# Gated linear attention and a low-rank mixer on one core: the second batch in whole chunks, the first batch's u transposed in PSUM, and a new order

## The chip, the cores and the metric

The kernel runs on one core of one Trainium2 chip. The time is device microseconds of one execution, and the number compared is the median of several. The engines are named as the profile names them: PE is TensorE, DVE is VectorE, ACT is ScalarE, POOL is GpSimd, SP is SyncE, which here only issues DMAs.

## The reference

For four batches, eight heads, 768 steps and head size 48, a recurrent state is decayed and updated at each step and read by the query. The result, laid out as (batch, step, 384), goes through a low-rank mixing over the steps (rank 32) and then a two-layer MLP with a residual:

```
state = alpha[:, :, t, :, None] * state + k_t v_t^T
y[:, :, t] = q_t state
h = (x^T U V)^T                       # x = y as (4, 768, 384)
u = x + h
out = u + max(u @ w_ch1, 0) @ w_ch2   # 384 -> 1536 -> 384
```

## The kernel before

**The recurrence.** The steps of a batch are cut into six chunks of 128. In a chunk, ACT takes Ln of alpha (`ln`), PE sums it over the steps (`cum`, or `pcum`), ACT takes Exp of the sum and of its negative (`exp`, twice) and of the total (`tot`, `ptot`). POOL or DVE scale k and q with these (`rk`, `rq`), PE transposes them (`tr`) or a DMA does (`tkq`, batch 3), PE forms the scores (`sc`, `psc`), DVE masks them, and PE multiplies them with v and adds the part from the state (`y`, or `pyi` and `py`). The state goes on through `d`, `add` and `st`. A *paired* chunk works on half of the heads for 256 steps, two steps to a partition, so that its loads read runs of 384 bytes where a whole chunk's read 192. `PAIRS` says how many blocks of 256 steps of each batch are paired: before, three in batch 0 and two in batch 1. Paired chunks have their own forms of the steps (`stage_pair`), whole chunks theirs (`stage_gla`).

**The mixer.** `stage_mix` forms x^T U (`xu`, copied out as `utx`), multiplies it with V for each chunk (`hb`), adds x on DVE (`u`), and transposes u into `uT`, by PE and a copy (`utr`, `uev`) in batches 0 and 1, by DMA (`tu`) in batches 2 and 3. `mlp1` multiplies w_ch1 with `uT` in 24 groups of three matmuls of 384 columns (two halves of the steps, twelve groups of outputs); each group fills a PSUM bank, which a `relu` on ACT or DVE empties. `mlp2` takes twelve matmuls per chunk; DVE adds u (`out`), and a DMA stores.

**The order.** PSUM has eight banks, and each step that makes PE results takes one. All steps of all batches are listed first (`Plan.add`), each with its number; then `Plan.run` issues them in the order of `TABLE`, three characters for each entry: two for the number of the step, one for its engine (P, A, D, G, S); `++` puts filler matmuls on PE. `SLOTS` gives the buffers. The framework's own scheduling is off, so each engine works in the order of `TABLE`, and the batches run into each other: the recurrence of the next batch lies between the MLP matmuls of the present one. One of the steps, listed last, is

```
P.add("table", lambda e: nc.scalar.preload_act_table_set("natural_log_exp_and_others"))
```

It names the set of ACT's function tables that has both Ln and Exp. In the `TABLE` of before it is ACT's third entry, behind two DMA issues.

Of the kernel before, what the change touches and what calls it, by code (L numbers as in the profile page):

```python
# [15 lines left out]
TABLE = """  # L16
ArA++BAASAvSA-AA3SQPAAySAsSCLA++BCNPAtSAzA++BA5ACOACPAAwS++BCiADSAECAAxSBAACRGAuS++BCSGCjACQACkPA4SClA++BCmAA7ADUPDVADWA
A0SC5ACTPCoGCUPCWABDSDXAEEPEGAA6SCpDA9ACVDCxPC7P++BCnACMAC9AAFGC+ABBSDrAA2SCyDCqPCsDCaPBHSCbDCXPCzPEFAA8SCrPCYDDtPCtAA1S
CcPCZDCeP++BCdDC8ADYGDaPCuPDZDCfPEIGDcAC-GDTGCwDEKPEHAAJPDbPC0DBCABFSABSDhPGCAAKADwA++BChACvDDiPDdDDjDEJGDvADuAA+SDePDgD
AGPELPAHADkPEMDC1PDfDBEAENABGSC2PBLSC3DDyGD0PD2ABISCgDBJSBKSBPSGEPDlDC6GGGADIPDJPDKDEOPDxGDLPDAGGHAEDGDBPC4DDzPDnPERPEPD  # L20
GFAAMSDMDALGDCPDDADmPDoPEQDESPD1AAQSDEABMSGJGDpAD3PGZAETDD5DDFPEUPDGDGIGDqAGbPDNPEVPGDGDOPD6P++BDsAGcADHDEWPEXAD4DD7PD8D
DPPDRAEYDGKPGMAD9PAYSGLPGNDACGADPD+PD-PEADGRPGSDDQAAEAEBAGOPGPDEZPEaPBTSGfGGwAGeAGdAEbAGyPG1ABNSGTD++BG0AEqPGQDBRSEoPGhP
GVPErDEkPGgGGWPGzABQAEcPEiPGjAEpDElDGiPGaGEsPHJAAUSAOGGXAEePEjDEtAAPGGkDGYAEdDHLPBOSHMAHNAEfDEmPGlPEnDANGGoPEgPGpDFGPGmD
GqDFHDFIPATABVSGnDFKPARGEhAFLAEwPExAASGFMPFNAE4PE2PAaGFQPE5DEyPBXSG2GBUSAZAFRDAbAFAPFJAE0PAcSE3ABSABZSFEPFFAGrDHOAG4PG6A
G3DHPDE1DFBAEuPHRPHTDFOPHQGEzDFPDG5PHiAFcPAXAFaPEvDG7AFdAAVAHSPHUDGsPGtPGuDBYSGvAG8PG+DAWGAhSBWSGxGGUGBaSAmSHVPBfSBrSG-P
FbAHkPHmAHoAFWPHADHBGE6PHXDH4AHnAFSPHlAG9DHqGFYPFTDH6PE7DH7AH8AHWDE+PHsPHuDHCDHpGE8PHKAFXAFZAHrPHtDFUPFVABbSE-AE9DHEPAgA
HFPHGPHYPHZDAfGBtSBjSHHDHvPHdPHIDHwDH+GIAPFCPAeGHaGAdAH9GHePFePHbDAiABcSHcDHxDICDFDAFkPF2PH-PIBDF8PIDPAlAHfPAjGAkGF9PBeS
HgAFwPBhSIFDHDGIEDHjABnSHyPH2PH3AH5AHzDH0DF3PFlPH1DIGPHhAApAFfPIHAIIPFxPIJAIQPISPAoGIKPAnGIRDITDAqGF+PFyPILDIMPINDFgPIYP
IZDF-DFzDF4PKCAKEPLBABkSIWPKFABzSJuAIXDIUPIOPIVAIPDKXAFmPFnDIaPBqSIbDJwPJxAF5DJ1DIiPKZPJvAIjAKdAI0PBlSFhDKGABdSAIGJyAJEP
JFABvSB1SIgPKKGJ2GI1AI+PI-AKIAIyPI4PKsAI5AIzAJGPIhDBiSI6PI7AJ0AJzAImPIqPKHAIrAInAKaAJKPIwPKDGJ+PJHAIkPKbAKuPKwAJIPLDPJLD  # L30
KcAKMPJ-DLWABwSJAPJJAIuPKyAJBAKfGIlDKeDKvAIxDBgSKJGLGAI2PI3DLHAIvAIcPLEABsSLIGIdAIePIfAKgPKiDJ3PBpSB0SIoPBmSJ5DLFAIpANFA
KxAIsPKhPItAJ4PKODKjAKSPKTDKLPJSPJTPJ6DBoSK0GJ7PLJGKNAB6SBySKUGKtGJ9DKkPKlDKPPKRDJUPLYPLZANHPKmDNJANKAKYGFqPFrPNNGKzGLKP
I8PNLAJ8DNIAKQDKnPBxSLaALcGKqPLMALLPLbDKoDKpGLNAB-SFsPK2PLdPK4DI9AKVPFtDK8PLfABuSK9DKrAJCPJDAK1PK3DLePNMGLgACDSK+GKAPKWA
JkPB3SB2SKBDB7SJVDB5SNWALOPNOSLPDK5PK6DLhPOMAJlPLQDK7DLCGLRPLSDLTGJmPNYPOOPCISORALXAN6ACESNbANoANcAJePLjDLUPLiDNaAK-PLAD
LVDJpPLkPJfPLlANZANPPNeGLmPLnAN8PN9ANGGN-ANQDJqPB4SLvPLtPN+ANRDOAANdGJrPCHSLwDOQALqPCCSLuDCASLxSLrDNXAOeALoPJYPLpDJMPNSP
NTDLsSJgPB8SJZPCFSL0PL1DJhDJsDJaPNqPNtALyPLzDCBSL2SJbDJNPJOPB9SB+SNsAJnDJPDOUGNjPNkDN7AL5PMNPNUPL6ANVDL3PNrAMDPMEANvDMOA
L4ANlGMFPOBDL9PMHPMIAOPAL-PMAAOCDODSNuAMGAOgPOhAL+AMLPMJPMKDMBPOTGOVSOiANwDMbPMTPCJSNfSMUAL7PMcDMfPMPPMCAMgDNpAMMAMVPMWD
MXPMYDOHPOSAOEPMhPOFDOjGL8DMjPMkAN1PN2DOGDOkGMdPMRPMSDNxSMZPCGSMQDMeDMnPN3GOIDOKPOJGOlSMoPMiAGBSOWPOLACKSNyPMaAOXDNgPFjS
NzDNhDNAPNBPMpPONAN0DOZPOmPNiDFpSN4PM2POaDM3POYDN5AOcPOdANmPMlPFvSObGOnDOfGOoDNnDOpPOqAMxPOrPOsAMyPGASMqDMrSMmDM4PO3PO4D
OyPO5PJWSFuSO0PO1DM7POtPNCPOzDO2SM8PM9PM5DO6DO7SOuDMzPM+DJdSOvPOwDOxSMsPMtPMuPPiPNDDPkPPoPPpAPaPPbAPcPPWPPXDPdDF0SM0DFiS  # L40
PMPPNAPCPPDDM1SPlANESPgPPjAPePPAPPGPPhDPOPPYPPBAPKPPLDPSPJoSPTAPUPPVDJjSMvDO8PJiSO9APEPPPDPHAPqPPrDPIPO+PPZAQFPJQSPfDQGP
QKPPmPMwSP7PP8PPnDQLPF7SJRSPFAM-SF1SO-DPxPQHPPJDPQPPRDM6SP2PP3PF6SP4PJcSP5DJtSFoSQMPQNDPsPPyPPzPJXSQIDQJSP0DP6SP1SQOSPtP
P9PP+DP-SPuPQAPQBPPvDPwSQCPQDDQES
"""
SLOTS = """
ABCDEFAAGHIAAJBCAKLAMAABNBBOCCCPBDBEAQBFARSGHACBBDTCUAEBDCVBBGAWEADXBBCEGACDCACBEAFAYZHACAFCCCaGBCAHDDbcBdBAAefghEDAGHDB
CBEAFGDAAEBBiCHABABFCDCEBABGFABCCCDHGFACBHBAGjACDCADAkABFlAEHACGCmBDDFCAABEACnAADGFBAHAECBADABGHAEFBBDDGHCFACDBBFEAHABCD
EGBEHABGEJFCHKEBGCDDBDAACEBCCHCAGECAADHFMEBDHBNOCAFCAGDCEBBLDCHDAGDIFPBAQDGBBBDGBEDGBEDRTAGBSEAUCDABAWFXEBYDADCABCZbBVCF
caHBACBFCCeHAAFCBHEEGAFBACBAAdEDDABfAGACgCEHBGhiDlACCAHECGACBkDDFmnDDAAGCHEBCAFACAABEGCFjBADDCBCBHEBCAGCDACFHACBEDFEGJHB
GFACHABECABBBDGHKBACMDBFAACBCEBBADEAGAEACOBEAICBALPCCAGBEAAVQGecACGZSfgCUhAFABCGBAADCECBCBFBBEDGCDBEBBACNCBFGDACEFDHBBAC  # L50
BFBAAXCCADDDHBlGFADECBAAHGDFEBHFBCCEGDHBaFACGBHFAkjBCEdGFAHBAiFHAFBGDEHABFHABHCGDEBAFEDCCnBGHH
"""
# [99 lines left out]
def kernel(  # L152
# [215 lines left out]
    def stage_pair(b, u, sprev, xb):  # L368
# [160 lines left out]

        def f_y(e):  # L530
            for h in range(HP):
                for j in range(2):
                    for c in range(2):
                        r = slice(64 * c, 64 * c + 64)
                        nc.tensor.matmul(  # L535
                            yb[c]()[:, h * D : (h + 1) * D], lhsT=pm()[r, (h // 2) * 2 + j, h % 2, :], rhs=rv()[r, HP * j + h, :],
                            start=(h == 0 and j == 0 and before[c] is None), stop=(h == HP - 1 and j == 1), skip_group_check=True,
                        )
# [286 lines left out]
    P.add("table", lambda e: nc.scalar.preload_act_table_set("natural_log_exp_and_others"))
# [31 lines left out]
```

## Time and profile before

| | |
|---|---|
| median of 3 runs | 158.62 us (157.86 to 159.13) |
| profiled execution, first to last instruction | 156.8 us |
| PE busy | 148.8 us, 1715 matmuls |
| DVE busy | 107.6 us, 236 instructions |
| ACT busy | 90.0 us, 234 instructions |
| POOL busy | 61.4 us, 95 instructions |
| DMA packets | 98291, of these 91968 under 512 B |

The profile's page gives only the span of the profiled execution; the median of the runs is 1.8 us longer than it. In the rows below, a group is a line of the kernel, an engine and an operation, the tile written and the tiles read, a count, then the busy time and the mean of one in ns, then the idle time of the engine ahead of them and what ended it. The chain is the work that ended last, followed back from the end; its pieces have a start, a length and a name. Rows of stretches give the length, and for each engine the busy time and the number of instructions, then the granted clock of PE, the DMA share and GB/s.

### The profile page before, as it was taken

To read this page: it belongs to the slowest core of one execution; us is meant where nothing else is said; L and a number is where in the kernel's file an instruction comes from. 1 tells how busy PE (TensorE), PEld (TensorE's weight loads), DVE (VectorE), ACT (ScalarE), POOL (GpSimd) and SP (SyncE) were. 2 spreads that over 40 slices of the span, in tenths; PEclk is the share of its full clock that TensorE was granted. 3 is DMA by queue.
4 is the path that set the end of the run, shared out by engine and by line. 5 is a ranking of instruction groups with operands and counts; after the bars stand their busy time and mean duration, and the time that the engine had idled before them with its cause. 6 is when DMAs were issued, how large, how long until landed. Compare 5 with 4: busy or idle time off the path is not lost.

```text
span 156.8 us, 4413 instructions
## 1 busy us (share of the span) xinstructions
PE 148.8 (95%) x1715; PEld 97.7 (62%) x1715; DVE 107.6 (69%) x236; ACT 90.0 (57%) x234; POOL 61.4 (39%) x95
## 2 busy tenths in 40 slices
PE   2878999999999999999999999999999999999992
PEld 0456678666767656666668666665667555556662
DVE  6038899987899628816588976885989580673162
ACT  3678889986978272999958585379232202450000
POOL 8285995756088600136679261052623000000000
PEclk9999999999999999999999999999999999999999
DMA  5999999999988989989989996897976346345625
GB/s 145 319 323 326 268 301 313 344 265 268 280 239 193 270 161 191 189 169 211 208 169 214 134 222 119 169 181 145 176 144 151 105 87 139 127 129 151 199 100 201
DMA packets 98291, 31.53 MB, mean 201 GB/s; under 512 B 91968, under 2 KB 98240, under 8 KB 98272
## 3 DMA queue, kind: packets, MB, share of 16 engines
q1 hardware_dynamic: 92464, 29.11, 80.6%
...
q14 instruction: 6, 0.05, 0.1%
...
## 4 chain that ended last, share of the span: by engine, by line
PE 84%; DMA 8%; DVE 4%; ACT 1%; issue 1%; ACTq 0%; DVEq 0%
PE ps L791 30%; PE ps L765 29%; DMA io<-in_alpha_dram 8%; PE ps L716 3%; PE ps L620 3%; PE ps L592 2%; PE ps L687 2%; PE ps L428 2%; PE ps L535 2%; PE ps L558 2%; PE ps L682 1%; PE ps L736 1%; PE ps L452 1%; PE ps L643 1%; PE ps L702 1%; DVE rkq L411 1%
## 5 line engine op out<-in xcount | busy, mean ns | idle before, releaser
L791 PE MATMUL ps<-w_sb,h1t 128*128 128x384 bf16 (+2 forms) x300 | 53.1, 319 | 0.0
L765 PE MATMUL ps<-uT,w_sb 128*128 128x384 bf16 x288 | 51.0, 326 | 0.1
L775 ACT ACTIVATE h1t<-ps 128x384 bf16<-128x384 f32 x58 | 27.2, 509 | 19.1 <-PE ps L765 19.0
L791 PEld LDWEIGHTS <-h1t 128*128 128x128 bf16 x300 | 27.3, 97 | 15.9 <-issue 0.6
L765 PEld LDWEIGHTS <-w_sb 128*128 128x128 bf16 x288 | 27.0, 98 | 16.3 <-issue 0.4
L777 DVE TENSOR_SCALAR h1t<-ps 128x384 bf16<-128x384 f32 x38 | 20.1, 552 | 19.4 <-PE ps L765 15.9
L579 POOL TENSOR_TENSOR rkq<-io,aa 128x384 bf16<-128x384 f32 x12 | 11.7, 975 | 23.0 <-ACT aa L569 13.2
L630 DVE TENSOR_TENSOR pm<-ps,maskc 128x512 bf16<-128x512 f32 x28 | 17.7, 681 | 2.8 <-PE ps L620 2.8
L717 DVE TENSOR_TENSOR ub<-xb,ps 128x384 bf16<-128x384 bf16 x24 | 12.2, 549 | 6.9 <-PE ps L716 6.9
L797 DVE TENSOR_TENSOR io<-ub,ps 128x384 f32<-128x384 bf16 (+2 forms) x25 | 12.9, 531 | 3.7 <-PE ps L791 3.6
L277 ACT CAST xb<-ps 128x192 bf16<-128x192 f32 (+1 forms) x21 | 8.2, 393 | 10.6 <-PE ps L687 7.9
L463 DVE TENSOR_TENSOR pm<-ps,maskp 128x512 bf16<-128x512 f32 x20 | 13.2, 682 | 0.5 <-PE ps L452 0.2
L277 ACT COPY kqt<-ps 128x512 bf16<-128x512 bf16 x18 | 10.5, 608 | 1.6 <-PE ps L428 0.8
L579 POOL TENSOR_TENSOR rkq<-io,ai 128x384 bf16<-128x384 f32 x9 | 8.2, 914 | 6.9 <-PE ps L643 3.9
L411 POOL TENSOR_TENSOR rkq<-io,ai 128x384 bf16<-128x384 f32 x9 | 8.5, 945 | 6.1 <-ACT lt L380 3.1
L568 ACT ACTIVATE ai<-ps 128x384 bf16<-128x384 f32 x14 | 7.0, 502 | 5.6 <-PE ps L560 3.1
L654 POOL TENSOR_TENSOR st<-sm,tot 128x384 bf16<-128x384 f32 x8 | 6.9, 868 | 8.2 <-DVE sm L670 8.0
L571 ACT ACTIVATE tot<-ps,off 128x4 f32<-128x4 f32 x22 | 5.6, 279 | 5.3 <-PE ps L560 3.4
L279 DVE COPY kqt<-ps 128x512 bf16<-128x512 bf16 x18 | 7.3, 417 | 1.4 <-PE ps L592 0.9
L428 PE MATMUL ps<-ident,rkq 128*128 128x128 bf16 x80 | 8.0, 228 | 0.1
L281 POOL CAST w_sb<-h1t 128x384 bf16<-128x384 f32 x14 | 6.8, 516 | 2.9 <-DMA h1t<-in_moe_w_ch_dram 2.9
L411 POOL TENSOR_TENSOR rkq<-io,aa 128x384 bf16<-128x384 f32 x7 | 6.4, 910 | 3.4 <-ACT aa L404 2.3
...
## 6 DMA issues: line engine op xcount, KB each, us to landing
...
```

The source lines that it names most:

```text
L277: nc.scalar.copy(dst, src)
L411: eng.tensor_tensor(jh(dst()[:, :, 0:D]), raw(a), jh(x()), op=ALU.mult)
L428: nc.tensor.matmul(dst, lhsT=ring()[:, HP * j + 2 * a : HP * j + 2 * a + 2, :].rearrange("t h w -> t (h w)"), rhs=ident, start=True, stop= ...
L463: nc.vector.tensor_tensor(dst, s2, maskp.to_broadcast([C, 2, 2, C]), op=ALU.mult)
L579: eng.tensor_tensor(dst()[:, :, 0:D], a(), x(), op=ALU.mult)
L630: nc.vector.tensor_tensor(pm()[:, :, par, :], s2, maskc.to_broadcast([C, HP, C]), op=ALU.mult)
L717: P.add(f"u {b}.{c}", lambda e, c=c, hb=hb: nc.vector.tensor_tensor(ub()[:, c, :], xb()[:, c, :], hb()[:, 0:DM], op=ALU.add), r=[hb] + xk( ...
L765: nc.tensor.matmul(hb()[:, 0:TW], lhsT=w1_sb[:, ct, jt * 128 : (jt + 1) * 128], rhs=u_half(uT, ct, tt, b in QUEUE_U), start=(ct == 0), sto ...
L775: nc.scalar.activation(dst, hb()[:, 0:TW], AF.Relu)
L777: nc.vector.tensor_scalar_max(dst, hb()[:, 0:TW], 0.0)
L791: nc.tensor.matmul(hb()[:, 0 : hi - lo], lhsT=h1()[:, jt, c * C : (c + 1) * C], rhs=w2_sb[:, jt, lo:hi], start=(jt == 0), stop=(jt == NJ - 1),
L797: P.add(f"out_{hi - lo} {b}.{c}", lambda e, hb=hb, lo=lo, hi=hi: nc.vector.tensor_tensor(flat(ou)[:, lo:hi], ub()[:, c, lo:hi], hb()[:, 0 ...
```

## The change

- `PAIRS` of batch 1 goes from 2 to 0: all its chunks are whole.
- Batch 0 (`INPLACE`) no longer forms u. x is transposed by matmuls with the identity into PSUM (`xt`), the low-rank part is added to the same bank by one more matmul (`ht`), and a copy makes `uT` of it (`xtev`). In the second MLP, a matmul of V and `utx` opens each bank (`hbo`), and `out` adds x where it added u.
- In paired chunks, `py` is two steps, one for each parity of the heads.
- `utx` has three buffers where it had two.
- `TABLE` and `SLOTS` are new.

```diff
-    PAIRS = {0: 3, 1: 2, 2: 0, 3: 0}
+    PAIRS = {0: 3, 1: 0, 2: 0, 3: 0}
+    INPLACE = (0,)
...
-    utxs = Pool(slots("utx", 2, [128, DM], BF16))
+    utxs = Pool(slots("utx", 3, [128, DM], BF16))
...
-        def f_y(e):
-            for h in range(HP):
+        def f_y(e, par):
+            for h in range(par, HP, 2):
...
-        P.add(f"py {b}.{u}", f_y, r=[rv, (pm, 0), (pm, 1)], w=[yb[0], yb[1]])
+        for par in range(2):
+            P.add(f"py {b}.{u}", lambda e, par=par: f_y(e, par), r=[rv, (pm, par)], w=[yb[0], yb[1]])
...
+        if b in INPLACE:
+            for tt in range(2):
+                for j in range(NCT):
+                    tb = Buf(bank)
+
+                    def f_xt(e, tt=tt, j=j, tb=tb):
+                        for n in range(NT):
+                            nc.tensor.matmul(tb()[:, n * C : (n + 1) * C], lhsT=xb()[:, tt * NT + n, j * C : (j + 1) * C], rhs=ident, start=(n == 0), stop=False, skip_group_check=True)
+
+                    P.add(f"xt {b}.{tt}.{j}", f_xt, r=[x for n in range(NT) for x in xk(b, xb, tt * NT + n)], w=[tb])
+                    P.add(
+                        f"ht {b}.{tt}.{j}",
+                        lambda e, tt=tt, j=j, tb=tb: nc.tensor.matmul(tb()[:, 0:TW], lhsT=utx()[:, j * C : (j + 1) * C], rhs=ve_sb[:, tt * TW : (tt + 1) * TW], start=False, stop=True, skip_group_check=True),
+                        r=[utx, ("ve", tt)], w=[tb],
+                    )
+                    P.add(f"xtev {b}.{tt}.{j}", lambda e, tt=tt, j=j, tb=tb: copy(e, uT()[:, j, tt * TW : (tt + 1) * TW], tb()[:, 0:TW]), r=[tb], w=[(uT, "t", tt, j)])
+            return utx
...
+            if b in INPLACE:
+                P.add(f"hbo {b}.{c}", lambda e, hb=hb, lo=lo, hi=hi: nc.tensor.matmul(hb()[:, 0 : hi - lo], lhsT=(ve_sb if paired(b, c) else vm_sb)[:, c * C : (c + 1) * C], rhs=utx()[:, lo:hi], start=True, stop=False), r=[utx, ("ve" if paired(b, c) else "vm", c // NT)], w=[hb])
...
-                            start=(jt == 0), stop=(jt == NJ - 1),
+                            start=(jt == 0 and b not in INPLACE), stop=(jt == NJ - 1),
```

What the new `TABLE` says can be read by counting the steps in the order in which `Plan.add` lists them. Fillers go from 11 to 5. DMA issues on ACT go from 11 to 16. ACT's Ln (L) and Exp (E) entries stand in these runs, with a bar where PE gets the first `mlp1` entry of batch 0, 1, 2 and 3:

```
before  TABLE L1 E2 L3 E5 L1 E5 L1 E3 L1 E6 L1 E1 L1 E5 L1 E2 | E1 L1 E2 L1 E4 L2 E1 L2 E1 |
        E4 L1 E7 L1 E6 L1 E7 L2 E1 L1 E1 L1 E8 L1 E2 | E6 |
after   L2 E1 L1 E2 L1 E9 L1 E2 L1 E4 L2 E6 L1 E2 | E3 L1 E3 L1 E5 L1 E3 L2 E7 L2 E3 L2 |
        E8 L1 E4 L1 E4 L1 E1 L1 E1 L1 E8 L1 E4 | E4 TABLE |
```

TABLE marks the `table` entry, 220th of ACT's 232 entries in the new order.

More of the change, by code (lines that the diff above doesn't have):

```diff
@@ L16 @@
 TABLE = """
[L17 to L40, printed above, removed]
@@ L41 @@
-PMPPNAPCPPDDM1SPlANESPgPPjAPePPAPPGPPhDPOPPYPPBAPKPPLDPSPJoSPTAPUPPVDJjSMvDO8PJiSO9APEPPPDPHAPqPPrDPIPO+PPZAQFPJQSPfDQGP
-QKPPmPMwSP7PP8PPnDQLPF7SJRSPFAM-SF1SO-DPxPQHPPJDPQPPRDM6SP2PP3PF6SP4PJcSP5DJtSFoSQMPQNDPsPPyPPzPJXSQIDQJSP0DP6SP1SQOSPtP
-P9PP+DP-SPuPQAPQBPPvDPwSQCPQDDQES
+AASA3ADVA++CDXPAvSCjAClPAFGAJPDYAArSA4SAGPA5SCLACNPDZADbDCmADdPDcGDePAzSC7AC9PDaACPAAKDCOACQACoAAwSCpGAHDAtSCSGC-AAuSCMG
+DgDAySCkGCnADfDDAADhPDiDDjD++CCyPCrPA-SC+AEHAEJPCUPCWAAsSEKACRGCzDA6SA0SDBGDWGELACtDA1SDCGC0PC1DA7SDvACaPCbDCTPCVD++BDDP
@@ new lines @@
+DFDDkPDlPDmDCcPCXPCZDDEPCdDCYDCePAxSA2SDnPC8ADGAEMADxPBBSCqGCsPDoDDHPDIDBASD0ADKPEOGDLPDMDENGCfPCgPA9SDyACuAA8SD1GDzAD2G
+ChAEQPEPPDQPDNPERACiADPPDJDA+SCvPBCSESDDRPDSPDUADTAEZPDODETPDpPBDSEIGD3PCxDCwDD4PGOAEVDEUDBHSD5ADqPEWPEXPEYDDrPDsPGQPD+P
+DtDAIGD6AGiADuAD7PD8DEaPBFSABSEbPDwGD-PEADC2PC3PC4PGSAGUAGTAGRAC6AC5AEcPEBPGkPACGADPECPAEAD9DEDPEEPGnAEGAEFAGlAElPBESGVG
+EdDEfPGXPEeDEgPEhAGWDAYSAaAGZDEuPGYPAMSAPGErPEoPGaDEsPEvPEtAEmPBLSG3AEpPEqAAZGEwDEiPGmAExPEyPEzDAOGEjPEkDGbPG5PG6AANAAbG
+FgPFhABGSG8AG9AAUSAWGFePGcDFiPFOPEnDFGPBJSAVGBPSFHDBMSAXGGoAFIPE0PE4PGqGFfAFPDFjAHMAFKPE1DG7AE5DGdDFAPHOPGPAGePFBDFLAGfD
@@ new lines @@
+BISBKSFYPFJAFMPHPAGgPHSAG+GGpDBTSHhAE2PFZDHAPFNAHRAE3AHQAGrPFcPFdDGtDGjAGsPGuDBNSG-GHCAAQSATGHjPHnAFaPFbAARGHBPHDDASGBQS
+GyPHmAFEPFFABOSHlAGhABXSBRSH2AGzDHkAGvPGwDHEPHGDFQPE6PFUPFRDE7AHTGHVPE8PG4AFVAFSPFTAE+PH4PH5AALGHUGHFDFCPHWPE9DG0GHXDHKP
+BUSHoGH6AFDAAcSAfAE-AAgGFWPGxDAeGBZSF5PBVSAdAFXAHLDH8GFrPHYDHqPHHPBYSHZPHbDHaDAhSG1PBWSBSAFsPGHPGIPAmAH+PHpDG2AHIDHrPHtD
+IAAAiAAjAF6PH7GHsDH9PH-DFkPFlPIBPICDBaSHuPHvDHwDAkGAlGFmPF7PGJPHJDHNAHcPHdDHeDHiGHxPHyDHzDIDDBbSBfABhAFtPHfPBjSBcSApAFyP
+FzPF0PAnABrAAoGBnSAqGFnPH0PHgDH3GIEPJ8AB3SFoDBgSFuPGAPBdABuSBvSH1DIFAIGPIHDFvDF8PF9DJoAJqPJuAJrAIUPIVDGKPIWPIXDGLDIQPJ+P
@@ new lines @@
+BpSIOPIPDF1PBiAJ-AKAAKBAIYPIIPIRDGBPJtAKCABoAKmAF2DIJDIZAK7AIKPILDGCPISPGDPKoPBkSBeAB5SKEGJsAKpAKDGITDIMPINDKsAKGPKIDKFP
+KHDLQAKRAIyPIzAImPGEDIiPInDIcPB-SBsSKrAJwGK9PK-AJ9GKtGJpGJvDIjDKqAKuGJyPIdALSPI+PI6PI2PI3DIoPBwSIaPLAAI-DJ0DJCPJ4PK+ALBA
+J5DIwPBlSI7AIpALTALUAIxDJDDNQAIkPB6SBtSBxSKMPKwPKvPKxDKNDIlAKTPJxPJzDIbAI0PI8PKVAKZGIsPKUACHAKYGI1AKWAKXAKyDKOGI9DLWGItA
+KJPBqSKKDJ1PJ2DKLDKzPBmSN0AJ3DBySIgPIhAIuPIvACCSJGPB2SIePNSPNUALCGNVAK0DIfDLYPIqPIrAI4PK1DI5ACASGMSBzSKbPKPPKaPKdDCFSKcD
+JPPLaDLDGKSGLVGJHAJ6PJ7DKQDFxSB0SB7SJEPB4SKhPKiDNAANWANTAB+SB1AJQPLXPLZDKjDJAPLFPLHAJBAKnGK2PNRGK3DK4GLEPLGDJFAJRPJSDK5P
@@ new lines @@
+LbPLIPM-ACBALdDKePGNSCGSK6AJKPJLPJMPNBPKfDB9ANEAKgDKkPLcDLJDLRGOYANCANiANFAN2PN5ANDAKlANYGK8GLLPNXGNZSJUPLKDLOPJVPN4ANGG
+LMDLNDLePLPDJIPJJANMPOaPOcACDSLfDJNDNdPLgPLhAObANNDNeDNfDJZPNHGJaPN3ALuPN6ALvDLnPLoDLiPN8GJWPNjGOGALjDLsPLtDJXDJjPLpPNkP
+NISNmANlANnANoALqDLkPJbPLlDJcDJkPJlPNaPNJPN7GN9SN+PJePNcDOADJmDOIPJfPNbDJgPLrSLwSMbPNKDNLDLmSB8AOKANgPMJPOJAN-DNqGMKDL1P
+MZPL5PL2DMcDMXPMYDL6DCJSCESNhAMaANOPNPDOLACIANpGNvPJhDJTSNrSMFPOOGMHPMDPMEAONDLxPOHGLyAMGAOdGOeGLzPL9PL+AFpSMPPMQDMfPMgA
+L7PL8DL3PMRPN1AMIAMSAMNPL4AOBPOTPMLPMdPMMANwDMTPMOAMUANxDOEPOCDF-SOFAODDOUDOPSOMAL0AMeDMBPMCDMVPMWDNsPNtDOfSOQPOSDOgPOhD
@@ L44 @@
+ORDL-PM6PM7PMAAMwPMrPCKSOZAOiDOVGOWPOjPNuDOkANyPNzDM1PMxPOXAJYSOlPOmAMsPMyPMzDOuPOnPOvDM8PM9DM0SOsPF4SOtDOwSOpPOqDOxPM2P
+OyDQJAMhPMiPMmPMnPOzPOoDOrSM3PMjPMoPO0DJnSMpDO1SMtPMuDM4DM5SJdSO+PO-DPGPO8PFwSO9AO2PPAPPkPO4PO5AMkDFqSPUPPaPPbAMlSPYPPZD
+PBDPVAPcPPSPPTDPgPPHAPdAPCPJOSMvSJiSPIPPQPO6PPJDPOPPDDPMPPePPPDPhDO3DPfDPKPPLDPRAP1PF+SGGSPNAPiPPWPPEPF3SPjAPXAPlAPFDP-P
+QAPQBPO7APwPPmPPnPPoPPpDPrPPqSM+SPsPPxPPyPQCDPzDP0SQEPQFPQGPQHDPtPPuDP2PP3PP6PQDSMqSGFSQISPvSP4DP5SP7PP8PP9DP+S
 """
 SLOTS = """
-ABCDEFAAGHIAAJBCAKLAMAABNBBOCCCPBDBEAQBFARSGHACBBDTCUAEBDCVBBGAWEADXBBCEGACDCACBEAFAYZHACAFCCCaGBCAHDDbcBdBAAefghEDAGHDB
@@ L47 @@
[L47 to L51, printed above, removed]
+AAABBBCACDDECEAABFGFAHABCBCGBHCCIAAJBADCDAAEGKABFBBLBAMNDCBCOPCHCBDADGECBHBDAQRDCGSHCDCTBFCBDEUCVACAHCGBEWFDXHCABYEGBDAC
@@ new lines @@
+ZDEFBGABDCAFaACEBAAADAGEDBBbBCHAAGFEDAcCHBCFEGCCAdCDBHFBefgCABDADCHFDGBhiABADBCjBECAHGBCAkCBAEFlGHmBBnACACCACFEAGHCADEBG
+BHBFCADEBBCDCGDDAHFFECBBEGDCBEACBFCEAHHBCDECACAHBBIJKBLNCMPHDEAORQBSTVFBUXBHDAEAFYAGWEZCACFDbCaBBEGAcfeCCBCBDBFACEAGdHCg
+hDDBBACAFEBGACjHADABCADkBCBGilnCFEAABDGAABHAmDDCECABDFCGABACBHDEFDBADCACHFEGGDHCHABEFCJIGKEBAAPQHCCFDDDBABEMBHFDCCSBEGVA
+FCLDBACBCCEBCBDGAHDBCBACGFDAZbBCCBCADGAABFCAEABNDEACCCAFfCBHEDFAGCAWBCABOBDCADAHEFCkcBDDgHnBEBACFDCDGCFEGCCFEACGBHBCAABA
+EFAHCCGCBBDAEFAChBCEBGDHAlBECBGAHABFGjAiHAAEGFCDFHBEDBHEAFDBAEBFAHGEBAGHCeCTKGm
@@ L535, in f_y @@
                         nc.tensor.matmul(
-                            yb[c]()[:, h * D : (h + 1) * D], lhsT=pm()[r, (h // 2) * 2 + j, h % 2, :], rhs=rv()[r, HP * j + h, :],
+                            yb[c]()[:, h * D : (h + 1) * D], lhsT=pm()[r, (h // 2) * 2 + j, par, :], rhs=rv()[r, HP * j + h, :],
                             start=(h == 0 and j == 0 and before[c] is None), stop=(h == HP - 1 and j == 1), skip_group_check=True,
@@ L756, in mlp1 @@
             hb = Buf(bank)
-            if b in QUEUE_U:
+            if b in INPLACE:
+                need = [(uT, "t", tt, j) for j in range(NCT)]
+            elif b in QUEUE_U:
                 need = [(uT, "c", c) for c in ((0, 1), (1, 2))[tt]]
@@ L779, in mlp1, with mlp2 @@
             P.add(f"relu {b}.{tt}.{jt}", g, r=[hb], w=[(h1, tt, jt)], after=casts[jt] if b == 1 else ())
-    def mlp2(b, ub, h1, c):
+    def mlp2(b, ub, h1, c, xb, utx):
         tt = c // NT
@@ L786, in mlp2 @@
             hb = Buf(bank)
+            if b in INPLACE:
+                P.add(f"hbo {b}.{c}", lambda e, hb=hb, lo=lo, hi=hi: nc.tensor.matmul(hb()[:, 0 : hi - lo], lhsT=(ve_sb if paired(b, c) else vm_sb)[:, c * C : (c + 1) * C], rhs=utx()[:, lo:hi], start=True, stop=False), r=[utx, ("ve" if paired(b, c) else "vm", c // NT)], w=[hb])
             for g in range(3):
@@ L792, in f @@
                             hb()[:, 0 : hi - lo], lhsT=h1()[:, jt, c * C : (c + 1) * C], rhs=w2_sb[:, jt, lo:hi],
-                            start=(jt == 0), stop=(jt == NJ - 1),
+                            start=(jt == 0 and b not in INPLACE), stop=(jt == NJ - 1),
                         )
                 P.add(f"mlp2_{hi - lo} {b}.{c}.{g}", f, r=[(h1, tt, jt) for jt in range(4 * g, 4 * g + 4)] + [("w2", jt) for jt in range(4 * g, 4 * g + 4)], w=[hb])
-            P.add(f"out_{hi - lo} {b}.{c}", lambda e, hb=hb, lo=lo, hi=hi: nc.vector.tensor_tensor(flat(ou)[:, lo:hi], ub()[:, c, lo:hi], hb()[:, 0 : hi - lo], op=ALU.add), r=[hb, (ub, c)], w=[(ou, n)])
+            P.add(f"out_{hi - lo} {b}.{c}", lambda e, hb=hb, lo=lo, hi=hi: nc.vector.tensor_tensor(flat(ou)[:, lo:hi], (xb if b in INPLACE else ub)()[:, c, lo:hi], hb()[:, 0 : hi - lo], op=ALU.add), r=[hb] + (xk(b, xb, c) if b in INPLACE else [(ub, c)]), w=[(ou, n)])
             if paired(b, c):
@@ L819 @@
                 whole = [(x, 0, x)]
-        stage_mix(b, xb, ub, uT)
+        utx = stage_mix(b, xb, ub, uT)
         mlp1(b, uT, h1, 0)
@@ L823 @@
         for c in range(NC):
-            mlp2(b, ub, h1, c)
+            mlp2(b, ub, h1, c, xb, utx)
     P.add("table", lambda e: nc.scalar.preload_act_table_set("natural_log_exp_and_others"))
```

## The prediction

> **What bounds the kernel now.** I read the page's first part, then the chain, then the busy time by stage. The stages are cut where TensorE begins the first MLP of the next batch (L765), at 32.9, 64.7, 102.3 and 130.5 us.
>
> ```profile
> span 156.8 us, 4413 instructions
> ...
> PE 148.8 (95%) x1715; PEld 97.7 (62%) x1715; DVE 107.6 (69%) x236; ACT 90.0 (57%) x234; POOL 61.4 (39%) x95
> ...
> PE 84%; DMA 8%; DVE 4%; ACT 1%; issue 1%; ACTq 0%; DVEq 0%
> ```
>
> ```profile
> core 0: us, PE busy (x) PEld busy (x) DVE busy (x) ACT busy (x) POOL busy (x), PEclk, DMA share, GB/s
> 0.00:32.90 32.90, 27.79 (x515) 19.34 (x516) 23.43 (x71) 25.73 (x68) 23.01 (x44) 1.00 1.06 293
> 32.90:64.70 31.80, 31.75 (x369) 20.88 (x368) 24.97 (x53) 21.22 (x53) 12.81 (x21) 1.00 0.98 228
> 64.70:102.30 37.60, 37.60 (x417) 25.16 (x415) 26.80 (x53) 27.82 (x79) 17.95 (x23) 1.00 0.95 180
> 102.30:130.50 28.20, 28.20 (x265) 17.60 (x263) 21.47 (x40) 10.40 (x26) 7.68 (x9) 1.00 0.75 139
> 130.50:156.80 26.30, 23.48 (x157) 14.71 (x154) 10.89 (x22) 4.85 (x11) 0.00 (x0) 1.00 0.49 150
> ```
>
> TensorE sets the time: it holds 84% of the chain, and from 32.9 us on it is busy without a gap until about 2.8 us before the end (26.30 less 23.48: the last add and store). ScalarE (ACT) is busy 57% and carries 1% of the chain. In the three stages that hold the recurrence (0 to 102.3 us) it is busy 25.73, 21.22 and 27.82 us, so it has 7.2, 10.6 and 9.8 us to spare, 27.6 us in all. The granted clock is 1.00 throughout.
>
> **The change part by part.** The largest term is in the order. ACT runs 24 Ln and 84 Exp activations, whose functions it looks up in a loaded table. The `table` entry loads one set that has both; before, it is the third entry of ACT's queue, ahead of the first Ln, and the trace has exactly one load:
>
> ```profile
> L825 ACT ACT_TABLE_LOAD x1 | 1.3, 1283 | 1.8 <-issue 1.8
> ```
>
> ```profile
> 0.73 1.01 ACTq L350 DMA_DIRECT2D io<-in_alpha_dram  x2
> 1.78 1.28 ACT L825 ACT_TABLE_LOAD   x1 [1.78 <-issue]
> 3.72 0.52 ACT L380 ACTIVATE lt<-io 128x384 bf16<-128x384 f32 x1 [0.66 <-DMA io<-in_alpha_dram]
> ...
> 5.25 0.49 ACT L403 ACTIVATE ai<-ps 128x384 bf16<-128x384 f32 x1 [1.00 <-PE ps L396]
> 5.63 0.48 ACT L404 ACTIVATE aa<-ps 128x384 bf16<-128x384 f32 x1
> ```
>
> In the new table the `table` entry stands 220th of 232 on ACT, behind the last Ln and Exp. Nothing else holds a set in place, and the schedule is manual, so the order written is the order issued. The builder, which is software, follows the program and puts a load ahead of each activation whose function the set then loaded lacks; it takes the lowest-numbered set that has the function, and for Ln that is a set without Exp, for Exp one without Ln. So every change between Ln and Exp in ACT's queue becomes a load. The runs listed under the change give 38: 14 ahead of batch 0's first MLP, 11 more ahead of batch 1's, 13 more ahead of batch 2's. The 39th is the entry itself, late, where ACT has room.
>
> Price of one: 1.283 us, and 0.11 us of overlap that back-to-back activations have (the one at 5.25 takes 0.49, the next starts 0.38 later): 1.39 us. ACT's own work per instruction is (90.0 − 1.3) / 233 = 0.381 us. ACT issues, besides DMAs, 57, 64 and 57 instructions in the three stages of the new order:
>
> - stage 0: 57 x 0.381 = 21.7, and 14 x 1.39 = 19.5, sum 41.2 us (now 32.9 for everything)
> - stage 1: 64 x 0.381 = 24.4, and 11 x 1.39 = 15.3, sum 39.7 us (now 31.8)
> - stage 2: 57 x 0.381 = 21.7, and 13 x 1.39 = 18.1, sum 39.8 us (now 37.6)
>
> That is 120.7 us of ACT up to batch 2's first MLP, where TensorE now arrives at 102.3. ACT becomes the bound of these stages. TensorE can't run ahead much: it has eight banks, each first-MLP bank leaves through a relu on ACT or VectorE, and SyncE's queue has `tkq 3.3`, which waits for batch 3's Exps, ahead of the `tu 2` transposes that batch 2's MLP reads. GpSimd's `rk` and `rq` wait behind the same Exps.
>
> Behind that point TensorE has the same left as now, 28.20 + 23.48 = 51.7 us, then 2.8 us of tail. ACT's queue starts at about 1 us. So 1.0 + 120.7 + 51.7 + 2.8 = 176.2 us if ACT never waits. How long it waits isn't in the trace: at least −4 us (TensorE leads by eight banks of three matmuls of 384 columns, 8 x 0.49, the L716 row below), at most the 27.6 us that it spares now. The nearest row is the present bound, TensorE, which waits 5.1 us in stage 0 and 0.05 in stage 1; I take 6 us. Span 182.2 us. The median of the runs, 158.62, is 1.8 us over this profiled span, so the time is **184.0 us**.
>
> The Trainium skill, "ScalarE: Activation LUTs", section "What ACT_TABLE_LOAD costs", gives the load about 1283 ns and adds a drain of about 1380 ns for every switch. The trace has the 1283; the sum by the page would be 38 x 1.38 = 52 us more, some 230 us (an estimate). Behind the one load the trace has 0.66 us of idle, which the alpha DMA ended, so no row shows a drain.
>
> The other edits are small. TensorE's pace in back-to-back work comes from the chain:
>
> ```profile
> 30.51 0.34 PE ps L736 x6
> ...
> 31.01 0.16 PE ps L389
> 31.17 0.08 PE ps L390
> 31.25 0.08 PE ps L391
> 31.34 0.01 PE ps L392
> 31.34 0.10 PE ps L396 x4
> ...
> 42.16 0.57 PE ps L452 x32
> 42.73 0.28 PE ps L486 x8
> ...
> 43.27 0.08 PE ps L560 x4
> ...
> 45.32 0.16 PE ps L558
> ...
> 47.56 0.30 PE ps L535 x16
> ...
> 48.04 0.29 PE ps L620 x8
> ...
> 54.17 0.17 PE ps L643 x4
> ...
> 54.51 0.20 PE ps L687 x8
> ...
> 58.22 0.49 PE ps L716 x3
> ```
>
> *Batch 1 in whole chunks.* Four paired chunks cost TensorE 0.43 (L389 to L396) + 0.285 (half of 0.57) + 0.28 + 0.30 = 1.30 us each, where the two forms differ; a whole chunk costs 0.16 + 0.08 + 0.29 + 0.17 + 0.20 = 0.90. Four times 0.40 is 1.6 us less. The 16 loads of these chunks go from runs of 384 bytes to runs of 192, 8192 packets more:
>
> ```profile
> DMA packets 98291, 31.53 MB, mean 201 GB/s; under 512 B 91968, under 2 KB 98240, under 8 KB 98272
> ```
>
> The DMA share is 0.95 to 1.06 up to 102 us, so this could cost something: nothing if bytes count, and if packets count the time of 16 loads again, 16 x 192 KB at 293 GB/s, 10.7 us. These loads are wanted in stage 1, which ACT enters about 9 us later than now; I take nothing, and if that cover is gone, up to 10.7 − 9 = 2 us.
>
> *Batch 0's u.* TensorE loses six `hb` (0.163 each) and three `utr` groups (0.34), 2.0 us, and gains 18 `xt` matmuls of 128 columns (nearest row L736, 0.056 each; L391's 192 columns, 0.08, is the upper end), 1.0 to 1.5, six `ht` and six `hbo` of 0.163, 2.0: about 1.0 us more. TensorE's sum is −0.6 us, and it isn't the bound while ACT is. VectorE loses six adds:
>
> ```profile
> L717 DVE TENSOR_TENSOR ub<-xb,ps 128x384 bf16<-128x384 bf16 x24 | 12.2, 549 | 6.9 <-PE ps L716 6.9
> L277 ACT COPY uT<-ps 128x768 bf16<-128x768 bf16 x3 | 2.4, 806 | 0.3 <-PE ps L736 0.3
> L277 ACT CAST utx<-ps 128x384 bf16<-128x384 f32 x4 | 2.0, 491 | 1.8 <-PE ps L702 1.8
> ```
>
> It gives back 6 x 0.549 = 3.3 us and one 0.55 copy, and takes four `xtev` of about 0.55; ACT swaps two `uev` of 0.806 for two `xtev` of 0.49. One add of 0.55 leaves the path from `xu` to the first MLP. Splitting `py` by parity lets half of it start one mask earlier, at most 0.68 us a chunk; the third `utx` buffer removes a reuse that no wait shows; six fillers fewer are worth 6 x 0.22 of TensorE in gaps. All of it hides behind ACT, so I cost it at nothing.
>
> **The rivals.** *The loads vanish in ACT's idle time.* A load waits for nothing, as the one at 1.78 us shows, so it can run while the next activation waits for its bank; for it speaks that ACT idles 43% now. Against it: 27.6 us spare and 18 fewer instructions (6.9 us) don't hold 37 x 1.39 = 51 us. With no wait left and TensorE's 4 us lead, 172 us of span, **174 us**.
>
> *Each load stops ACT for longer than itself*, since the activation before must be out and the next must fill the pipe. The row bounds it at 0.63 us (the gap to the alpha landing); 38 x 0.63 = 24 us more, **208 us**.
>
> *One load serves, and the order keeps its promise* (the other side). The decider is whether the set loaded first holds both functions; then ACT has 82 us of work and TensorE binds again. 158.6 − 0.6 (TensorE) − 0.55 (the add) = **157.5 us**. The Trainium skill, "ScalarE activation tables: per-element evaluation and per-set limits", section "Table sets in the compiler and the runtime", says that the back end picks the longest run per block, which would give this one load. For it speaks the single load of the trace, against it that this load sits exactly where the kernel's own entry asked for it, behind two issues.
>
> **How the numbers follow.** Forecast with some waiting (178 to 195 us): 0.66. Loads absorbed as far as they can be: 0.13. Longer stops: 0.12. One load: 0.07, which splits into 0.03 faster by over 1% and 0.04 within 1% (about what a measurement of this kernel can tell from no change). Something else: 0.02. The range goes from 171 (absorbed, less a little) to 207 (waits as long as now, 176.2 + 27.6 + 1.8 = 205.6); it leaves out the one load, most of the longer stops and the rest, 0.18.
>
> **What would show it.** ACT_TABLE_LOAD x39 near 1.28 us; ACT busy some 130 us; the chain's ACT share far above 1%; TensorE with gaps that ACT ends in the first 125 us and none behind; L765 of batch 2 starting near 127 us. A single ACT_TABLE_LOAD would make the prediction wrong at once; 39 loads with the span under 170 would mean that TensorE runs further ahead of ACT than eight banks allow.

## The result and the profile after

The changed kernel takes 193.37 us (median of 4 runs, 191.61 to 194.25), the kernel before, beside it, 158.38. The ratio is 1.2174, with a 95% interval of 1.2086 to 1.2261. The prediction said 184.0 us, in a range of 171 to 207. Executions more than 1.5% above the fastest of the same kernel are left out of the times and ratios below (two of four in `before_table_late`, one each in `after_table_first`, `after_table_stage2` and `after_first_runs384`), and the profiles of the first two kernels named are of such an execution, at 206.70 and 169.85 us.

The page of the changed kernel, its first part, the clock by slices, and the chain:

```profile
span 192.2 us, 4242 instructions
...
PE 160.0 (83%) x1624; PEld 102.9 (54%) x1624; DVE 111.9 (58%) x240; ACT 131.9 (69%) x254; POOL 62.2 (32%) x98
...
PEclk9999978889996999999879999969999999999999
...
PE 55%; ACT 36%; issue 5%; DMA 1%; DVE 1%; ACTq 0%; DVEq 0%
```

ACT's busy time went from 90.0 to 131.9 us and its share of the chain from 1% to 36%. The groups of ACT, with their count and mean, name what was added:

```profile
L552 ACT ACT_TABLE_LOAD x14 | 18.0, 1283 | 0.2
...
L570 ACT ACT_TABLE_LOAD x7 | 9.0, 1283 | 1.6 <-PE ps L561 1.6
...
L380 ACT ACT_TABLE_LOAD x5 | 6.4, 1283 | 1.3 <-PEq L863 1.2
L572 ACT ACT_TABLE_LOAD x5 | 6.4, 1283 | 1.4 <-PE ps L561 1.4
...
L403 ACT ACT_TABLE_LOAD x2 | 2.6, 1283 | 0.0
L405 ACT ACT_TABLE_LOAD x2 | 2.6, 1283 | 0.0
L569 ACT ACT_TABLE_LOAD x2 | 2.6, 1283 | 0.0
...
L404 ACT ACT_TABLE_LOAD x1 | 1.3, 1283 | 0.0
L847 ACT ACT_TABLE_LOAD x1 | 1.3, 1283 | 0.0
```

There are 39, each 1.283 us, on the lines of Ln (L380, L552) and Exp, and one from the `table` entry itself (L847). Here is one pair in ACT's timeline:

```profile
4.12 0.52 ACT L380 ACTIVATE lt<-io 128x384 bf16<-128x384 f32 x1
4.67 1.28 ACT L403 ACT_TABLE_LOAD   x1
5.96 0.49 ACT L403 ACTIVATE ai<-ps 128x384 bf16<-128x384 f32 x1
```

The load begins 0.03 us after the activation before it ends, and the next activation begins 0.01 us after the load: 1.42 us from where the activation would have begun with the usual overlap. The busy time by stage, cut as before at the first MLP of each batch:

```profile
0.00:43.20 43.20, 29.87 (x426) 20.24 (x427) 21.65 (x65) 36.19 (x67) 21.34 (x43) 0.92 0.97 240
43.20:87.40 44.20, 38.22 (x387) 24.98 (x384) 28.38 (x56) 36.47 (x73) 16.31 (x23) 0.96 0.84 176
87.40:137.20 49.80, 39.93 (x405) 25.04 (x402) 31.84 (x63) 42.94 (x80) 20.15 (x27) 0.93 0.69 135
137.20:165.60 28.40, 28.36 (x260) 17.87 (x261) 19.07 (x37) 10.92 (x24) 4.46 (x6) 1.00 0.53 115
165.60:192.20 26.60, 23.59 (x158) 14.81 (x155) 10.98 (x23) 5.34 (x12) 0.00 (x0) 1.00 0.39 129
```

All of the time went into the first three stages: they grew by 10.3, 12.4 and 12.2 us, and the last two by 0.2 and 0.3. In the first three TensorE, busy without a gap from 32.9 us on before, is now idle for 13.3, 6.0 and 9.9 us. That is 24.0 us more of idle time than before; the other 10.9 us of the growth are TensorE being busy for longer, 108.0 us in these stages against 97.1.

### The profile page after: what moved, and what is told of

Same layout as the page of the kernel before. It is cut to its first block, busy times and chain, and to the rows that moved or that the text cites. A ratio compares the mean times of both kernels' runs of the same rounds, so it can differ in the third digit from the quotient of the medians.

```text
span 192.2 us, 4242 instructions
## 1 busy us (share of the span) xinstructions
PE 160.0 (83%) x1624; PEld 102.9 (54%) x1624; DVE 111.9 (58%) x240; ACT 131.9 (69%) x254; POOL 62.2 (32%) x98
## 4 chain that ended last, share of the span: by engine, by line
PE 55%; ACT 36%; issue 5%; DMA 1%; DVE 1%; ACTq 0%; DVEq 0%
PE ps L813 22%; PE ps L785 18%; ACT L552 6%; ACT L570 3%; ACT L572 3%; ACT lt L552 3%; ACT L380 3%; ACT h1t L795 3%; PE ps L593 2%; ACT aa L570 2%; PE ps L644 2%; ACT ai L569 1%; PE ps L621 1%; DMA io<-in_alpha_dram 1%; PE ps L688 1%
## 5 line engine op out<-in xcount | busy, mean ns | idle before, releaser
L785 PE MATMUL ps<-uT,w_sb 128*128 128x384 bf16 x288 | 54.3, 337 | 5.7 <-ACT aa L570 1.8
L580 POOL TENSOR_TENSOR rkq<-io,aa 128x384 bf16<-128x384 f32 x16 | 14.9, 934 | 40.3 <-ACT aa L570 25.8
L631 DVE TENSOR_TENSOR pm<-ps,maskc 128x512 bf16<-128x512 f32 x36 | 22.8, 683 | 3.5 <-PE ps L621 3.5
L279 DVE COPY kqt<-ps 128x512 bf16<-128x512 bf16 x27 | 10.8, 420 | 12.5 <-PE ps L593 5.2
L735 DVE TENSOR_TENSOR ub<-xb,ps 128x384 bf16<-128x384 bf16 x18 | 9.1, 549 | 3.2 <-PE ps L734 3.1
L644 PE MATMUL ps<-rv,rkq 128*128 128x96 bf16 x60 | 5.1, 218 | 6.7 <-ACT aa L570 4.9
L463 DVE TENSOR_TENSOR pm<-ps,maskp 128x512 bf16<-128x512 f32 x12 | 7.9, 686 | 4.7 <-PE ps L452 3.0
L570 ACT ACTIVATE aa<-ps 128x384 bf16<-128x384 f32 x18 | 8.8, 497 | 1.6 <-PE ps L561 1.5
L559 PE MATMUL ps<-lt,ut_ones 128*128 128x384 bf16 x18 | 6.0, 335 | 4.2 <-ACT h1t L795 2.2
L552 ACT ACTIVATE lt<-io 128x384 bf16<-128x384 f32 x18 | 9.3, 523 | 0.2
```

The lines of the kernel that those rows point to most:

```text
L279: nc.vector.tensor_copy(dst, src)
L552: P.add(f"ln {b}.{c}", lambda e: nc.scalar.activation(lt()[:, :, 0:D], at(), AF.Ln), r=[at], w=[lt])
L570: P.add(f"exp {b}.{c}", lambda e: nc.scalar.activation(aa().rearrange("t h d -> t (h d)"), cb()[:, 0:DM], AF.Exp), r=[cb], w=[aa])
L580: eng.tensor_tensor(dst()[:, :, 0:D], a(), x(), op=ALU.mult)
L631: nc.vector.tensor_tensor(pm()[:, :, par, :], s2, maskc.to_broadcast([C, HP, C]), op=ALU.mult)
L735: P.add(f"u {b}.{c}", lambda e, c=c, hb=hb: nc.vector.tensor_tensor(ub()[:, c, :], xb()[:, c, :], hb()[:, 0:DM], op=ALU.add), r=[hb] + xk( ...
```

## The experiments

**One entry moved to the front, and one moved to the back.** The theory was that the loads cost the time; the rival, that the rest of the change does. Both were tried at once: the changed kernel with `table` ahead of the first Ln, and the kernel before with `table` behind the last Exp. No step is changed, only the place of one entry of `TABLE`:

```diff
  after_table_first    (changed kernel)   ACT: pload_a 0.3; + table; ln 0.3; ...  utx 3; - table; relu 3.0.3
  before_table_late    (kernel before)    ACT: pload_a 0.5; - table; ln 0.0; ...  utx 3; + table; relu 3.1.10
```

> The changed kernel with one entry of the order moved: table ahead of the first Ln. Theory (the loads cost the time): one ACT_TABLE_LOAD instead of 39, ACT busy near 83 us, time 157.5 us (155.5 to 159.5). Rival (the new order, the whole chunks' smaller DMA runs or the new u are what is slow, and the loads hide): above 175 us.

> The kernel before with the table entry moved behind the last Exp, to the place that it has in the changed kernel. Its order has 38 changes between Ln and Exp too. Theory: 39 loads, ACT work 195 x 0.381 + 38 x 1.39 = 127 us up to the first MLP of batch 2, 1 + 127 + 54.5 = 183 us of span without a wait and some 195 us (185 to 205) with them. Rival (it is the rest of the change, and this order hides its loads): below 165 us.

The changed kernel with `table` first took 166.77 us, ratio 1.0495 (1.045 to 1.054) to the kernel before: 26.6 us less than with 39 loads. Its trace has one load:

```profile
L847 ACT ACT_TABLE_LOAD x1 | 1.3, 1283 | 1.2 <-PEq L863 1.2
```

The kernel before with `table` late took 203.61 us, ratio 1.2827 (1.2746 to 1.2908): 45.0 us more, inside the 185 to 205 that were expected. So the loads alone make either kernel slow. But 166.77 is neither the 157.5 of the theory nor the 175 of the rival: some 8 us of the change's loss are something else.

**Loads for one stage and for two.**

```diff
  after_table_stage1   table at batch 0's first mlp1: 14 loads ahead of it
  after_table_stage2   table at batch 1's first mlp1: 25 loads ahead of it
```

> The changed kernel with the table entry at batch 0's first MLP: 14 loads ahead of it, 15 in all. Theory (each stage pays for its own loads): stage 0 stays as long as in the changed kernel (43.2 us, 10.3 more than before) and the rest as with one load, about 168 us (163 to 172). Rival (the loads of the start are caught up later, since TensorE's order has slack behind): below 162 us.

> The changed kernel with the table entry at batch 1's first MLP: 25 loads ahead of it, 26 in all. Theory: stages 0 and 1 stay long (10.3 and 12.5 us more than before), about 180 us (174 to 185). Rival (stage 1's loads hide behind TensorE, and the loss sits in stage 2): about 168 us.

With 15 loads the time was 173.40 us (ratio 1.0926, 1.0876 to 1.0976), with 26 it was 185.01 (1.1633, 1.156 to 1.1706). The first lies above its range of 163 to 172 and the second at the top of 174 to 185, since both had been counted up from the theory's 157.5 us and not from 166.77. From 166.77 up to 193.37, stage 0's 14 loads cost 6.6 us, stage 1's 11 cost 11.6, stage 2's 13 cost 8.4. A load cost 0.47, 1.06 and 0.64 us of time, always less than the 1.42 us that it held ACT. Stage 0's part is the one that missed: 6.6 in place of 10.3. With 15 loads TensorE began batch 0's first MLP at 42.6 us, with one at 32.1, so some of the late start is made up later, as the rival had it.

**ACT work in place of loads.** Is it the time that a load holds ACT, or something that the reload does? The changed kernel with `table` first got small copies at each of the 37 later changes between Ln and Exp:

```diff
+    P.busy = lambda: [nc.scalar.copy(scr, scr) for _ in range(6)]      # 4 in the second run
...
+                if f and f != now:                                     # f: "L" for ln, "E" for exp, tot, ptot
+                    if now:
+                        self.busy()
+                    now = f
             op.fn(...)
```

> The changed kernel with table first, and at each of the 37 later changes between Ln and Exp six small copies on ACT (128x160 in place, data that nothing else reads) ahead of the activation, in place of the load: about 1.3 us of ACT that waits for nothing. Theory (a load costs what it holds ACT, nothing more): ACT busy near 130 us and a time within 5 us of the changed kernel's 193 us. Rival (the reload does something beside that, a drain or a stall that the profile does not show): below 185 us at the same ACT busy time.

> As the run with six copies, with four in place of six. Six held ACT for 2.00 us at a change (an activation that would start at 5.29 us starts at 7.29), four should hold it 1.33 us, where a load held it 1.42 (5.96 less 4.54 us): 37 x 1.33 = 49 us of ACT against 54. Theory (a load costs what it holds ACT): 187 to 193 us, a few us below the changed kernel. Rival (a load does something more): below 183 us.

Six copies took 218.10 us (ratio 1.3792, 1.376 to 1.3825). That hit neither side: the copies, each waiting for the one before, held ACT 2.00 us at a change and not the 1.3 that I had set out to give. So the dose was sized by that trace, and four copies took 189.73 us (1.1971, 1.1905 to 1.2037). The timeline of the run with four:

```profile
4.72 0.52 ACT L390 ACTIVATE lt<-io 128x384 bf16<-128x384 f32 x1 [0.18 <-DMA io<-in_alpha_dram]
5.15 1.37 ACT L260 COPY scr<-scr 128x160 bf16<-128x160 bf16 x4
6.43 0.48 ACT L413 ACTIVATE ai<-ps 128x384 bf16<-128x384 f32 x1
```

An activation that could begin at 5.15 begins at 6.43, 1.28 us. By what was held: 37 x 1.28 = 47 us of ACT cost 23.0 us of time, the loads' 38 x 1.42 = 54 us cost 26.6, and 37 x 2.00 = 74 us cost 51.3. At the price of the four copies (0.49 us of time for each us held) 54 us would cost 26.2, and the loads cost 26.6; between 54 and 74 us the price rises to 1.2 per us. Within the spread of the runs a load costs what it holds ACT, and no more.

**The other 8 us: the runs of 192 bytes.** The loads of batch 1's first four chunks were given back their 384-byte runs in the changed kernel with `table` first, and in the kernel before they were given the 192-byte runs.

```diff
  after_first_runs384
-            if paired(b, c):
+            if paired(b, c) or (b == 1 and c < 4):     # in stage_loads only
  before_runs192
-            if paired(b, c):
+            if paired(b, c) and b == 0:                # in stage_loads only
  before_runs192_half
+            if paired(b, c) and (b == 0 or c < 2):
```

> The changed kernel with table first, and the 16 loads of batch 1's first four chunks read in runs of 384 bytes as before (each tile gets other rows of the same arrays, so the output of batch 1 is not the reference's; bytes, issues and all else are the same). Theory (the 8 us that are left after the table is put first are the price of the 192-byte runs): 159 to 161 us. Rival (they come from the new order or the other edits): 166 to 167 us.

> The kernel before with the same 16 loads read in runs of 192 bytes (wrong rows for the paired steps, output of batch 1 not the reference's), nothing else changed. Theory (the runs cost it): 163 to 168 us. Rival (the order of before hides slower loads, or the run length does not matter): 158 to 160 us.

With the longer runs the changed kernel took 159.65 us (ratio 1.0108, 1.0072 to 1.0144), 7.1 less. With the shorter ones the kernel before took 164.62 (1.0403, 1.0378 to 1.0429), 6.5 more. The two agree, one with the new order and one with the old, so it is the runs and not the order. The stretches show where; first the kernel before, then with 192-byte runs (the last column is GB/s):

```profile
20.00:30.00 10.00, 9.78 (x251) 7.41 (x250) 9.75 (x25) 9.39 (x27) 7.25 (x12) 1.00 1.10 325
30.00:40.00 10.00, 9.95 (x106) 6.67 (x105) 8.47 (x18) 7.75 (x19) 6.12 (x11) 1.00 1.10 262
```

```profile
20.00:30.00 10.00, 9.78 (x251) 7.34 (x249) 9.76 (x25) 8.88 (x26) 6.00 (x10) 1.00 0.81 163
30.00:40.00 10.00, 7.72 (x84) 4.73 (x82) 6.53 (x14) 5.81 (x13) 3.54 (x8) 1.00 0.98 257
40.00:50.00 10.00, 8.72 (x115) 5.84 (x116) 6.93 (x15) 7.29 (x20) 5.47 (x9) 1.00 1.02 238
50.00:60.00 10.00, 8.70 (x116) 5.60 (x115) 7.44 (x17) 5.65 (x14) 5.03 (x9) 1.00 1.01 263
```

From 20 to 30 us the transfers bring half of the bytes, at a smaller DMA share (0.81 against 1.10), and TensorE, before without a gap from 32.9 us on, is then idle for 4.9 us between 30 and 60 (2.28, 1.28 and 1.30). Behind these loads on SyncE's queue stand the MLP's weights. Of the idle time 2.3 us end with a cast of weights (1.34 by POOL, 0.95 by ACT), and by the chain another 1.4 (0.96 and 0.40) with what ACT does right behind such a cast. These are the issues of the weight loads (L320), by source line, with their count and the first and last start, before and then with 192-byte runs:

```profile
L320 SPq DMA_DIRECT2D h1t<-in_moe_w_ch_dram x7: 488/989/3558, 21.8 to 44.5; - x7
```

```profile
L320 SPq DMA_DIRECT2D h1t<-in_moe_w_ch_dram x7: 490/906/3693, 27.1 to 53.0; - x7
```

The waits for what they bring (sum, count and longest, in us), in the same order:

```profile
POOL w_sb L281 <- DMA h1t<-in_moe_w_ch_dram: 2.9, 3, 1.5
```

```profile
POOL w_sb L281 <- DMA h1t<-in_moe_w_ch_dram: 14.5, 7, 3.8
ACT w_sb L277 <- DMA h1t<-in_moe_w_ch_dram: 7.6, 4, 2.8
```

The last weight load goes out at 53.0 us, 8.5 later, and the casts of the weights wait 22.1 us for their data, against 2.9. The chain shows what held the weights back. SyncE's issues (SPq) have no share of the chain of the kernel before; with 192-byte runs they have 18%. From 9.75 to 39.57 us it is one issue behind the other, 0.04 us apart, and then a weight load under way:

```profile
PE 64%; SPq 18%; DMA 14%; ACT 1%; issue 1%; ACTq 0%; DVE 0%
```

```profile
35.70 3.87 SPq L357
39.57 0.04 issue
39.61 5.56 DMA h1t<-in_moe_w_ch_dram
```

An issue that held SyncE for 0.51 us at 2.21 us held it for up to 3.87 here. Why the issues of the shorter runs take longer, no run separates.

The Trainium skill, "DMA: Bandwidth & Descriptors", section "Why small descriptors are slow (HBM only)", gives each packet about 3 cycles beside its 32-byte beats; by that two runs of 192 bytes cost 18 cycles and one of 384 costs 15, a fifth more (an estimate). The runs show the direction, but a larger delay than a fifth of the 10.7 us of these loads.

> The kernel before with the loads of batch 1's chunks 2 and 3 alone, 8 of the 16, read in runs of 192 bytes (wrong rows, output of batch 1 not the reference's). If each slower load costs its part, half of the 6.5 us that all 16 cost: 161 to 162 us. If the later ones hide behind TensorE's work or the earlier ones alone delay the rest of the queue: 158 to 159.5 us.

With the later 8 of the 16 loads alone the time was 159.82 us (ratio 1.0094, 1.0062 to 1.0126): 1.5 us, not half of 6.5. The earlier eight, or the backlog that all 16 make together, carry the larger part; which of the two wasn't tried.

**SyncE's issues moved to ACT.** If SyncE's issue time were the limit, spreading the issues should help.

```diff
  after_first_issue_act: 12 of the first 38 loads in TABLE, every third, engine S -> A, at the same places
```

> The changed kernel with table first, and 12 of the first 38 loads issued by ACT's queue instead of SyncE's, at the same places of the order. If SyncE's issue time is what holds the loads back (it issues without a break to 36 us there), at least 3 us faster, 160 to 164 us. If the transfers themselves are the limit, within 1 us of 166.8.

It took 191.66 us (ratio 1.2126, 1.2079 to 1.2172), 25 us slower, which neither side had. The issues on ACT stand behind activations that wait, in ACT's own order. In this kernel's stretches, with the clock before the last two columns:

```profile
30.00:40.00 10.00, 5.75 (x96) 4.54 (x97) 4.46 (x9) 1.35 (x4) 5.20 (x8) 0.60 1.04 236
40.00:50.00 10.00, 5.38 (x95) 3.39 (x94) 2.54 (x6) 5.16 (x16) 0.00 (x0) 0.50 0.39 73
50.00:60.00 10.00, 9.02 (x65) 5.70 (x66) 4.25 (x9) 5.82 (x17) 4.07 (x8) 0.70 0.10 20
```

```profile
36.31 0.37 ACTq L357 DMA_DIRECT2D io<-in_alpha_dram  x1
...
47.30 0.38 ACTq L357 DMA_DIRECT2D io<-in_k_dram  x1
...
57.30 0.37 ACTq L357 DMA_DIRECT2D io<-in_q_dram  x1
```

Loads that belong to batch 1's first chunks go out at 36, 47 and 57 us, and the transfers then run at 73 and 20 GB/s. As a test of SyncE's issue time this run says nothing, since it changed when the loads go as well as who issues them. That SyncE's issues are on the path is read from the chain above; what faster issuing would bring stays open.

**The second part alone, and the split alone.** `before_u_in_psum` is the kernel before with batch 0 in `INPLACE` and its order adapted; `before_py_split` splits `py` in place.

```diff
  before_u_in_psum
-    hb 0.c (PE), u 0.c (DVE), utr 0.c (PE), uev 0.c (ACT, DVE)
+    xt 0.t.j, ht 0.t.j (PE, where hb stood), xtev 0.t.j (DVE, where u stood), hbo 0.c (PE, ahead of mlp2 0.c)
  before_py_split
-    py b.u
+    py b.u (parity 0); py b.u (parity 1)
```

> The kernel before with the second part alone: batch 0's transposed u built in PSUM and its low-rank part added in the second MLP bank, batch 1 still paired, the order of before with xt and ht where hb stood, xtev where the adds stood, utr and uev dropped, and hbo ahead of each chunk's first second-MLP matmuls. By the prediction's terms TensorE has about 1.0 us more and the path to the first MLP is shorter by an add and a transpose: 157.5 to 159.5 us, no change that can be told. Rival (this part is what costs the 8 us): above 163 us.

> The kernel before with py in two halves by parity, one behind the other at the place of the one, and nothing else. By the prediction at most 0.68 us a chunk where TensorE waits for the second mask; TensorE's gaps lie in the first 33 us alone: 157.3 to 158.4 us. Rival (two more waits on TensorE cost as much as they save): 158.4 to 159.

The u in PSUM took 159.56 us (ratio 1.0091, 1.0059 to 1.0124), a small loss of 1.4 us and just past the 159.5 of its range. TensorE's busy time in its profile is 1.1 us above the 148.8 of before:

```profile
PE 149.9 (95%) x1721; PEld 98.5 (62%) x1721; DVE 107.6 (68%) x235; ACT 88.6 (56%) x232; POOL 61.4 (39%) x95
```

The split took 158.16 us, ratio 0.9993 (0.9965 to 1.002): nothing. No version that was run beats the kernel before.

## Why the prediction was right, and where it was off

*The loads.* 39 were expected and 39 came, at 1.283 us; the price of a change was 1.42 us where 1.39 was taken. The drain that the Trainium skill's "ScalarE: Activation LUTs" adds in "What ACT_TABLE_LOAD costs" isn't there: 0.03 us ahead of the load and 0.01 behind it. The rival of longer stops falls with it, and the copies show the same by time. (That rival's bound was read as 0.63 us where its row has 0.66, which makes 25 us and not 24.)

*The place.* The last two stages were expected to stay at 54.5 us and took 55.0. The loss lies ahead of batch 2's first MLP, where it was put.

*ACT's waits, the term that was mis-sized.* The sum gave 1.0 + 120.7 + 6 = 127.7 us up to that point; it came at 137.2. The ACT work was right: 115.6 us busy, where the terms without the lost overlap give 178 x 0.381 + 38 x 1.283 = 116.6. The waiting was 15.5 us and not 6. It lies in all three stages, in which ACT stood idle for 7.0, 7.7 and 6.9 us (21.6 in all, of which some 5 are the start and the lost overlap that the sum had counted, and 1 is work below the sum); that stage 2 is furthest from its sum (49.8 us against 39.8) is in part work that slid into it, 15 loads where 13 were counted. I took the waits from TensorE as the bound of the kernel before, whose order kept it fed. In this order ACT waits for TensorE and TensorE for ACT. A stretch of stage 2:

```profile
119.81 0.65 PE L785 MATMUL ps<-uT,w_sb 128*128 128x384 bf16 x3
...
121.50 0.91 POOL L580 TENSOR_TENSOR rkq<-io,ai 128x384 bf16<-128x384 f32 x1 [4.45 <-DMA io<-in_alpha_dram]
...
124.86 0.49 ACT L570 ACTIVATE aa<-ps 128x384 bf16<-128x384 f32 x1
...
125.40 0.43 PE L644 MATMUL ps<-rv,rkq 128*128 128x96 bf16 x4 [4.95 <-ACT aa L570]
```

For these 4.95 us TensorE stands before `d 3.0`, while ACT goes through `exp`, `ln` and `tot` with a load ahead of each. The `rk` that `d` multiplies is there at 122.4 us, when POOL's row ends. But by `SLOTS` `d 3.0` writes the PSUM bank in which `cum 3.0` left its sum, and ACT's second `exp` of that chunk reads this bank until 125.35; the matmul starts 0.05 us later. So a late ACT stops TensorE through the banks that it has still to empty, and not through its results alone. Behind `d`, `xu 2` and `mlp2` wait for ACT as well (for the cast at 125.23 and the relu at 125.97). That such stretches make up the 15.5 us is read from this one, not shown by a run.

*The other edits, costed at nothing.* For the kernel with one load this step failed: the prediction's rival had 157.5 us, the run 166.77. The 16 loads of batch 1 were bounded at 0 to 10.7 us, taken as 0, with 2 us if the cover went; where one table load serves they cost 6.5 and 7.1. The cover was argued from when these loads are wanted. I didn't name what stands behind them on SyncE's queue, the weights of the MLP, which are wanted at 33 us. In the changed kernel itself the cover may hold: its chain has no SyncE issue, and its casts wait 5.4 us for the weights (3.6 on POOL, 1.8 on ACT), not the 22.1 of `before_runs192`. The u in PSUM was priced right in TensorE's time (1.0 us expected, 1.1 measured); where TensorE binds, it is 1.4 us of time, and whether it hides behind ACT in the changed kernel wasn't run. So without the loads the change is a loss too: 7.1 us of runs, and 1.1% left, where the second part alone makes 0.9%.

Taken away one behind the other, from 193.37 down to the 158.16 of the kernel before, the loads, the runs and the rest are 26.6, 7.1 and 1.5 us. Such steps add up in any order, but their sizes depend on it: in the order of before, the same 39 loads cost 45.0 us. How much of the runs' 7.1 us still shows while the loads are there wasn't run.
